# Token sums behind the attention output, both memory reciprocals in PSUM, K's last cast in halves

## The chip, the cores and the metric

The kernel runs on one core of one Trainium2 chip. The metric is the device time of one execution in microseconds. Before the change three runs took 749.27, 747.28 and 747.86 us, a median of 747.86.

## The reference

Two parts read the same x, 2048 tokens of 512 features, and a gate per token mixes them.

```python
def _A_ref(x, mem0, Wq, Wk, Wv, Wo, seg_len):      # 32 heads of 128, memory of 8 rows, segments of 32 tokens
    mem = mem0
    for s in range(n_seg):                          # 64 segments, one after the other
        h = jnp.concatenate([mem, xs], axis=1)      # 8 memory rows + 32 tokens
        q, k, v = ...                               # h times Wq, Wk, Wv
        scores = jnp.einsum('bhqe,bhke->bhqk', q, k) * scale
        scores = jnp.where(mask[None, None], scores, -1000000000.0)
        p = _softmax(scores, axis=-1)
        o = jnp.einsum('bhqk,bhke->bhqe', p, v)
        o = jnp.einsum('bhte,hed->btd', o, Wo)
        mem = o[:, :M, :].copy()                    # the next segment's memory
        outs.append(o[:, M:, :])
def _B_ref(x, w1, b1, w2, b2):
    y = _layernorm(x, axis=-1)
    h = _gelu(jnp.einsum('bsd,df->bsf', y, w1) + b1)
    return jnp.einsum('bsf,fd->bsd', h, w2) + b2
g = _sigmoid((x * gate_w).sum(-1, keepdims=True))
return g * a + (1 - g) * b
```

All weights and activations are bf16. The segments form a chain: segment s+1 needs the eight memory rows that segment s produced.

## The kernel before

The kernel has three stages. The first, to about 76 us, computes part B: layer norm, first matmul and gelu for all tokens, and the second matmul for seven of the sixteen blocks of 128 tokens. The hidden activations of the nine others are stored in DRAM (`h_dr`). The second stage is a loop over the 64 segments, here called steps 0 to 63; the last one leaves the loop half way. The third is the clean end: the last segment's output, sums that guard against overflow, and the last block of the result.

**One step.** The stationary operand `hT` has 32 columns: 24 tokens of the segment and 8 memory rows. The other 8 tokens of each segment ("left" tokens) depend on no memory, so for a whole block of four segments they are projected one block ahead, as side work. A matmul loads 32 columns of weights and uses one of four column groups of the array; four of them side by side are called a set here. A step on the matrix engine (PE) is:

1. Q and K in halves of 16 heads, order Q0, K0, Q1, K1 (`qk_unit`, L129), into the PSUM banks `U[0], U[2], U[1], U[3]`. ScalarE (ACT) casts each half to bf16 (`qk_cast`, L134), VectorE (DVE) transposes it into `QT` or `KT` (`qk_tr`, L138).
2. `scores(s, 0)` (L267, L271) of heads 0 to 15 into the bank `SbF`; ACT makes the exponentials `E` of them (L828).
3. V's first half into `X1` and one set of V's second half into `X2` (`v_unit`, L148); ACT casts V (`v_cast`, L834).
4. `xsums(E, 0)` (L715) sums the exponentials of the token queries over the keys; `msum(0)` (L816) does so for the memory queries of heads 0 to 15.
5. `scores(s, 1)` of heads 16 to 31 into `U[0]`, which need K1; the rest of V; `msum(1)` (L278, L281).
6. The attention output `av` (L291, L296): E times V, into all four `U` banks, first heads 0 to 15, then 16 to 31.
7. The memory rows' projection `wo_pass` (L160) into `X2`, cast to `w` (L752), and `new_mem` (L761), whose three results DVE casts into the next `hT` (L763).

Only the memory queries are normalised before `av`. `mnorm` on DVE reduces the sums (first half only, L823), takes the reciprocal (L824) and multiplies it into E's last 16 columns (L825). `RP` is the list of the two places where these reciprocals are kept: the first in the PSUM bank `SbF`, the second in the SBUF tile `RS`. The token queries are normalised behind `av`: `recip_x` takes the reciprocal of their sums (L726, L727), stores it to DRAM (`r_dr`, L730), reads it back broadcast to all partitions (`Rb`, L733), and in the next step GpSimd (POOL) multiplies it with the raw output (`x_norm`, L745) into `UT` and `UL`. `wo_pass` of that step needs this `UT`. Behind the reciprocal DVE also copies both `RP` into `R` (L735) and puts the mask back into `SbF` (L260).

**Side work.** PE is filled with work that is on no chain: the next block's left tokens or the last block's left projection (the generator `fill`, taken in units by `run(n)`: `W1` = 2 units before `av`, `W2` behind it, `W3` behind the projection, then one each between the parts of `new_mem`), and halves of the deferred second MLP matmul (`mlp_halves`, L689: 4 matmuls of 256 columns into the bank `W`), taken by `next(mlp)`. Each `hm` tile serves two halves. `hm_load` orders as many new tiles as have been used since the last call; it stands in `recip_x` between the store and the broadcast, on the same queue (SP). In step 2 the fill is MLP work alone, `mlp_units`, two halves to a unit.

**What sets the order.** The program is written out by hand (`manual_schedule`): each engine runs its instructions in the order of the source, and semaphores that the framework derives from overlapping tiles hold an instruction until what it needs is done. The SP queue takes DMAs in order too, and one that waits holds those behind it.

Of the kernel before, what the change touches and what calls it, by code (L numbers as in the profile page):

```python
# [9 lines left out]
FP32 = mybir.dt.float32  # L10
BF16 = mybir.dt.bfloat16
# [17 lines left out]
def kernel(ctx, tc, A_x, A_mem0, A_Wq, A_Wk, A_Wv, A_Wo, A_seg_len, B_x, B_w1, B_b1, B_w2, B_b2, gate_w, out):  # L29
    nc = tc.nc  # L30
    P = 128
# [100 lines left out]
    def qk_cast(bk):  # L132
        Tb = ew.tile([P, 8, 32, 2], BF16, tag="Tb", bufs=3, name="Tb")
        nc.scalar.copy(out=Tb[:], in_=bk.rearrange("p (a b e) -> p a e b", a=8, b=2))  # L134
        return Tb

    def qk_tr(Tb, dst, hf, c0=0):
        nc.vector.transpose(out=dst[:, 8 * hf:8 * hf + 8, c0:c0 + 32, :].rearrange("p a r b -> p a (r b)").bitcast(FP32),  # L138
                            in_=Tb[:].rearrange("p a e b -> p (a e b)").bitcast(FP32))
# [6 lines left out]
    def v_unit(bk, G, vb, kc):  # L146
        for j in range(4):
            nc.tensor.matmul(bk[32 * j:32 * j + 32, :], lhsT=G[:, kc, :], rhs=Wv5[:, kc, 4 * vb:4 * vb + 4, j, :],  # L148
                             start=(kc == 0), stop=(kc == KC - 1), tile_position=(0, 32 * j))
# [65 lines left out]
    def wo_left(T, bk):  # L215
        for n in range(NW):
            wo_group(bk, UL[T % 2], n)
            if n < NW - 1:
                yield

        def ca():
            wl = cw.tile([P, Dm], BF16, tag="wl", name="wl")
            nc.scalar.copy(out=wl[:], in_=bk[:])
            wls[T] = wl
        act_q.append(ca)
        yield
# [24 lines left out]
                              in_=QL[T % 2][:].bitcast(FP32).rearrange("p a (l s) b -> p a l s b", s=SPT)[:, :, :, si])  # L251


    RS = ep.tile([P, 32], FP32)
    RP = [SbF[:, 336:368], RS[:]]


    def mask_put(i2):
# [25 lines left out]
    def av(s, V, E):  # L284
        T, si = divmod(s, SPT)
        Uv = [U[j][:, 0:NG * 40].rearrange("p (i q) -> p i q", q=40) for j in range(4)]
        for i2 in range(2):
            for i in range(4 * i2, 4 * i2 + 4):
                for j in range(4):
                    q = slice(32 * j, 32 * j + 32)  # L290
                    nc.tensor.matmul(Uv[j][:, i, :], lhsT=V[q, i, :], rhs=E[q, i, 8:48],  # L291
                                     start=(i == 0), stop=False, skip_group_check=True, tile_position=(32 * j, 0))
            for j in range(4):
                q = slice(32 * j, 32 * j + 32)
                lo = slice(4 * i2, 4 * i2 + 4)
                nc.tensor.matmul(Uv[j][:, lo, :].rearrange("p i (a b) -> p i a b", b=8)[:, :, 0:5:4, :], lhsT=VP[T % 2][q, si, i2, :],  # L296
                                 rhs=E[q, lo, :].rearrange("p i (a b) -> p i a b", b=8)[:, :, 0:7:6, :],
                                 start=False, stop=True, skip_group_check=True, tile_position=(32 * j, 0))
# [329 lines left out]
    def run(n):  # L628
        for _ in range(n):
            next(fill, None)  # L630
# [5 lines left out]
    def side(T, si):  # L636
        gens = []
        if si == 2:
            gens = [wo_left(T - 1, X1) if T >= 1 else mlp_units(8)]
        elif T + 1 == NT:  # L640
            gens = [mlp_units(4)] if si < 2 else []
        else:
            gens = [[left_qk(T + 1, 0, 0, X1), left_qk(T + 1, 1, 0, U[3])], [left_qk(T + 1, 0, 1, X1), left_qk(T + 1, 1, 1, U[3])], [],
                    [left_v(T + 1, 0, X1), left_v(T + 1, 1, U[3])]][si]
        return chain(*gens)
# [32 lines left out]
    def mlp_outs():  # L678
        while outs:
            mlp_out(outs.pop())  # L680
# [16 lines left out]
    def mlp_units(n):  # L697
        for _ in range(n):
            next(mlp, None)
            next(mlp, None)  # L700
            yield
# [10 lines left out]
    def xsums(E, h):  # L712

        for c in range(4):
            nc.tensor.matmul(xs[32 * c:32 * c + 32, h, 0:40], lhsT=BO[:, 0:P:4], rhs=E[:, 4 * h + c, 0:40],  # L715
                             start=False, stop=True, skip_group_check=True, tile_position=(0, 32 * c))
# [51 lines left out]
    for s in range(nseg):  # L768
# [20 lines left out]
        for n, (t, hf) in enumerate(QK4):  # L789
            bk = U[(0, 2, 1, 3)[n]]  # L790
            for kc in range(n == 1, KC):
                qk_unit(bk, hc, t, hf, kc)
                if n == kc == 0:
                    qk_unit(U[2], hc, *QK4[1], 0)
            if n == 0:
                flush(act_q, 9)
                flush(dve_q, 9)
            qk_tr(qk_cast(bk[:]), (QT, KT)[t], hf, LEFT * (1 - t))
            if n == 0:
                mask_put(1)  # L800
        V = cx.tile([P, NG, Dh], BF16, tag="V", name="V")
# [9 lines left out]
        def msum(i2):  # L811
            if i2:
                sums(U[3][:, 320:352].rearrange("p (i q) -> p i q", q=8), E[:, 4:8, :], 40, 48, 8, True)
                return
            for j in range(4):
                nc.tensor.matmul(U[1][32 * j:32 * j + 32, 320:384], lhsT=BO[:, 32 * j:32 * j + 32], rhs=E[:, 0:4, 40:56],  # L816
                                 start=True, stop=True, skip_group_check=True, tile_position=(0, 32 * j))

        def mnorm(i2):
            r, e = RP[i2], E[:, 4 * i2:4 * i2 + 4, 40:56].rearrange("p i (a q) -> p i a q", q=8)  # L820
            if i2 == 0:
                m = U[1][:, 320:384].rearrange("p (i a q) -> p i q a", i=4, a=2)
                nc.vector.tensor_reduce(out=r.rearrange("p (i q) -> p i q", q=8), in_=m, axis=AX.X, op=ALU.add)  # L823
            nc.vector.reciprocal(out=r, in_=U[3][:, 320:352] if i2 else r)  # L824
            nc.vector.tensor_tensor(out=e, in0=e, in1=r.rearrange("p (i q) -> p i q", q=8).unsqueeze(2).to_broadcast([P, 4, 2, 8]), op=ALU.mult)  # L825
# [10 lines left out]
        v_cast(0, 0)  # L836
        v_unit(X2, hc, 1, 0)
        if not last:
            xsums(E, 0)
            msum(0)  # L840
            mnorm(0)
        scores(s, 1)
        exps(1, 0)
        v_cast(0, 1)
        exps(1, 1)
        for kc in range(1, KC - 1):
            v_unit(X2, hc, 1, kc)
        if not last:
            if s:
                next(mlp, None)  # L850
            msum(1)
            mnorm(1)
        v_unit(X2, hc, 1, KC - 1)
        for h in range(2):
            v_cast(1, h)
        if last:
# [1 line left out]
        run(W1)  # L858
        if s:
            next(mlp, None)  # L860
        xsums(E, 1)
        recip_x(s)
        av(s, V, E)
        for j in (0, 2, 1, 3):
            nc.scalar.copy(out=UT[s % 2][:, j, :, 0:M], in_=U[j][:, 0:NG * 40].rearrange("p (i q) -> p i q", q=40)[:, :, 32:40])  # L865
        x_raw(s)
# [15 lines left out]
        mlp_outs()  # L882
        for _ in fill:
            pass
        if si == 3 and T + 2 < NT:
            left_x(T + 2)
        flush(dve_q, 9)
# [9 lines left out]
    for _ in out_sel(T - 1, X1):  # L897
        pass
    fill = wo_left(T, X2)
    run(3)  # L900
    nc.vector.reciprocal(out=R[:, nx], in_=SbF[:, 0:32 * NG])
    nc.scalar.activation(out=rmin[:, nx], in_=R[:, nx], func=ACTF.Copy, accum_out=tot[:, 3:4])
    ws[s - 1] = wo_pass(UT[s % 2])
    Rr = R[:, nx].rearrange("p (i q) -> p i q", q=32)
    nc.vector.tensor_tensor(out=E[:, :, 8:40], in0=E[:, :, 8:40], in1=Rr, op=ALU.mult)
    nc.vector.tensor_tensor(out=E[:, :, 0:8], in0=E[:, :, 0:8], in1=Rr[:, :, 0:8], op=ALU.mult)
# [176 lines left out]
```

## Time and profile before

| | us |
|---|---|
| median of three runs | 747.86 |
| the profiled execution | 750.09 |
| its span, first to last instruction | 748.2 |
| PE busy | 732.8 |
| ACT busy | 536.7 |
| DVE busy | 448.9 |
| POOL busy | 246.6 |

One execution was profiled. Rows of the timeline give start, duration, engine, line, operation, output and inputs, shape and count of merged instructions, and in brackets how long the engine had stood idle and what released it. `DVE KT L138 <- ACT Tb L134` in the waits means that DVE's instruction of line 138 waited for ACT's of line 134. Matmul rows overlap: a row's duration is how long one matmul takes from end to end, and the pace is read from the distance of starts. PEld is the weight load that goes ahead of a matmul. Rows of `windows` give busy times per engine and, behind them, the share of full speed at which the matrix engine's clock was granted. A step lasts about 10.2 us.

### The profile page before, as it was taken

Reading aid. Unit: us, or ns where it says so; the run is one execution under the profiler, and the core shown is the slowest. Engines: PE = TensorE matmul, PEld = TensorE weight load, DVE = VectorE, ACT = ScalarE, POOL = GpSimd, SP = SyncE. Lnnn points to the kernel's source line nnn. Section 1 sums busy time; section 2 is a strip of 40 time slices with the busy share of each in tenths; the row PEclk is TensorE's granted clock in tenths of the full one; section 3 lists DMA queues with packets and bytes.
Section 4 is the critical chain, followed back from the end, with each engine's and each line's share of the span. In section 5 each row is a group of like instructions: output and inputs, shape, how many; then the busy total and the mean of one; then the engine's idle time right before and its main releaser. Section 6 shows DMA issues by size and latency. Waiting matters only on the chain. (4 is left out here: it accounts for less than half of the span.)

```text
span 748.2 us, 44010 instructions
## 1 busy us (share of the span) xinstructions
PE 732.8 (98%) x19147; PEld 428.8 (57%) x19147; DVE 448.9 (60%) x1541; ACT 536.7 (72%) x1629; POOL 246.6 (33%) x515
## 2 busy tenths in 40 slices
PE   8999998999999999999999999999999999999997
PEld 5776554556565555555555555555555555555553
DVE  6877554656565555656565665556665656555554
ACT  6777765777777777777777777777777777777664
POOL 4001332332334333343234334243333343333331
PEclk9999999999999999999999999999999999999999
DMA  8999222222222323122321323231322313222221
GB/s 308 343 360 360 84 83 55 69 87 80 78 68 62 97 74 93 47 83 80 93 79 38 96 75 97 69 81 57 92 78 82 85 44 94 69 90 70 85 63 61
DMA packets 61944, 76.82 MB, mean 103 GB/s; under 512 B 26729, under 2 KB 51922, under 8 KB 60210
## 3 DMA queue, kind: packets, MB, share of 16 engines
q1 hardware_dynamic: 60802, 72.51, 31.1%
q8 instruction: 151, 2.47, 1.3%
q0 software_dynamic: 400, 0.92, 0.3%
q10 hardware_dynamic: 544, 0.52, 0.2%
q14 instruction: 47, 0.39, 0.2%
HBM read 60.21 MB, written 7.70 MB: 91 GB/s over the span
## 5 line engine op out<-in xcount | busy, mean ns | idle before, releaser
L134 ACT CAST Tb<-U 128x512 bf16<-128x512 f32 x288 | 168.8, 586 | 82.5 <-PE U L129 76.8
L745 POOL TENSOR_TENSOR UT<-XR,Rb 128x384 bf16<-128x384 bf16 x126 | 114.1, 927 | 324.6 <-DMA Rb<-r_dr 228.0
L129 PEld LDWEIGHTS <-hT 128*32 128x32 bf16 x4096 | 108.8, 97 | 97.8 <-issue 2.0
L129 PE MATMUL U<-Wq_sb,hT 128*32 128x512 bf16 x2048 | 145.9, 382 | 0.4 <-DVE hT L763 0.4
L129 PE MATMUL U<-Wk_sb,hT 128*32 128x512 bf16 x2048 | 145.2, 381 | 0.0
L148 PE MATMUL X<-Wv_sb,hT 128*32 128x512 bf16 x2048 | 142.9, 378 | 0.0
L160 PE MATMUL X<-Wo_sb,UT 128*32 128x512 bf16 x2016 | 120.8, 380 | 0.0
L834 ACT CAST V<-X 128x256 bf16<-128x256 f32 x256 | 88.7, 372 | 16.0 <-PE X L148 1.1
L138 DVE STREAM_TRANSPOSE QT<-Tb 128x256 f32<-128x256 f32 x128 | 57.0, 445 | 71.1 <-ACT Tb L134 70.9
L763 DVE CAST hT<-U 128x8 bf16<-128x8 f32 x126 | 20.8, 167 | 130.9 <-PE U L761 96.6
L160 PEld LDWEIGHTS <-UT 128*32 128x32 bf16 x2048 | 56.4, 96 | 55.7 <-issue 16.6
L721 ACT CAST XR<-U 128x256 bf16<-128x256 f32 x252 | 78.6, 438 | 0.0
L752 ACT CAST w<-X 128x128 bf16<-128x128 f32 x189 | 44.8, 310 | 41.7 <-PE X L160 41.0
L138 DVE STREAM_TRANSPOSE KT<-Tb 128x256 f32<-128x256 f32 x128 | 57.0, 445 | 25.9 <-ACT Tb L134 25.9
L737 POOL TENSOR_TENSOR racc<-racc,R 128x128 f32<-128x128 f32 x63 | 28.8, 457 | 105.7 <-DVE R L735 101.1
L148 PEld LDWEIGHTS <-hT 128*32 128x32 bf16 x2048 | 45.2, 95 | 20.6
L689 PE MATMUL W<-w_sb,hm 128*32 128x256 bf16 x728 | 50.5, 273 | 3.6 <-DMA hm<-h_dr 3.6
L865 ACT CAST UT<-U 128x64 bf16<-128x64 f32 x252 | 35.4, 227 | 25.9 <-PE U L296 25.9
L745 POOL TENSOR_TENSOR UL<-XR,Rb 128x128 bf16<-128x128 bf16 x126 | 51.5, 430 | 0.0
L809 ACT ACTIVATE E<-U 128x64 bf16<-128x64 f32 (+1 forms) x128 | 35.0, 273 | 9.3 <-PE U L271 0.4
L484 PEld LDWEIGHTS <-w_sb 128*128 128x128 bf16 (+1 forms) x352 | 34.1, 100 | 10.4
L160 PE MATMUL X<-Wo_sb,UL 128*32 128x512 bf16 x512 | 38.7, 379 | 1.0 <-POOL UL L896 1.0
(184 smaller groups left out, 1250.5 us busy)
## 6 DMA issues: line engine op xcount, KB each, us to landing
Rb<-r_dr SPq DMA_DIRECT2D x63, 512.0 KB, 3.9
Wv_sb<-in_A_Wv_dram SPq DMA_DIRECT2D x4, 1024.0 KB, 7.5
Wq_sb<-in_A_Wq_dram SPq DMA_DIRECT2D x4, 1024.0 KB, 8.5
Wk_sb<-in_A_Wk_dram SPq DMA_DIRECT2D x4, 1024.0 KB, 8.4
Wo_sb<-in_A_Wo_dram SPq DMA_DIRECT2D x4, 1024.0 KB, 12.6
VP<-VL SPq DMA_DIRECT2D x64, 64.0 KB, 3.7
hm<-h_dr SPq DMA_DIRECT2D x91, 32.0 KB, 2.6
c<-c_dr SPq DMA_DIRECT2D x16, 128.0 KB, 4.6
```

The source lines that it names most:

```text
L129: nc.tensor.matmul(bk[32 * j:32 * j + 32, :], lhsT=G[:, kc, :], rhs=W5[t][:, kc, h0:h1, j, :], start=(kc == 0), stop=(kc == KC - 1), tile_ ...
L134: nc.scalar.copy(out=Tb[:], in_=bk.rearrange("p (a b e) -> p a e b", a=8, b=2))
L138: nc.vector.transpose(out=dst[:, 8 * hf:8 * hf + 8, c0:c0 + 32, :].rearrange("p a r b -> p a (r b)").bitcast(FP32), in_=Tb[:].rearrange("p ...
L148: nc.tensor.matmul(bk[32 * j:32 * j + 32, :], lhsT=G[:, kc, :], rhs=Wv5[:, kc, 4 * vb:4 * vb + 4, j, :], start=(kc == 0), stop=(kc == KC - ...
L160: nc.tensor.matmul(bk[32 * c:32 * c + 32, :], lhsT=U_[:, j, i, :], rhs=Wo_sb[:, 4 * i + j, :], start=(n == 0), stop=(n == NW - 1), tile_po ...
L689: nc.tensor.matmul(W[32 * c:32 * c + 32, cc], lhsT=hm[:, 32 * c:32 * c + 32], rhs=w2_sb[:, fc, cc], start=(fc == 0 and h == 0), stop=(fc = ...
L721: nc.scalar.copy(out=XR[:, j], in_=U[j][:, 0:NG * 40].rearrange("p (i q) -> p i q", q=40)[:, :, 0:32])
L745: nc.gpsimd.tensor_tensor(out=out[:, :, 4 * h:4 * h + 4, o:o + b - a], in0=XR[:, :, 4 * h:4 * h + 4, a:b], in1=Rb[:, h, :, :, r:r + b - a] ...
L752: nc.scalar.copy(out=w[:, a:b], in_=bk[:, a:b])
L809: nc.scalar.activation(out=E[:, 4 * i2:4 * i2 + 4, c], in_=Sb[i2][:, :, c], func=ACTF.Exp, scale=scale)
L834: nc.scalar.copy(out=V[:, i0:i0 + 2, :].rearrange("p i e -> p (i e)"), in_=(X1, X2)[vb][:, 256 * h:256 * h + 256])
L865: nc.scalar.copy(out=UT[s % 2][:, j, :, 0:M], in_=U[j][:, 0:NG * 40].rearrange("p (i q) -> p i q", q=40)[:, :, 32:40])
```

## The change

- The second memory reciprocal is kept in `SbF` next to the first; the tile `RS` is gone.
- K1 is cast and transposed in two halves of eight heads each, both casts first, then both transposes.
- `xsums(E, 0)` moves from before `msum(0)`, and `xsums(E, 1)` from before `av`, to behind `av`; `recip_x` follows them there.
- The last set of V's second half moves ahead of `msum(1)`; the MLP half that stood before `msum(1)` moves behind it.
- The fill of step 2 has six units, not eight; one MLP half is added at the end of step 3 and three at the end of step 4.
- In the clean end three sets of the leftover projection move from before the last `wo_pass` to behind it.

```diff
-    RS = ep.tile([P, 32], FP32)
-    RP = [SbF[:, 336:368], RS[:]]
+    RP = [SbF[:, 336 + 32 * i:368 + 32 * i] for i in range(2)]
...
-            gens = [wo_left(T - 1, X1) if T >= 1 else mlp_units(8)]
+            gens = [wo_left(T - 1, X1) if T >= 1 else mlp_units(6)]
...
-            qk_tr(qk_cast(bk[:]), (QT, KT)[t], hf, LEFT * (1 - t))
+            if n < 3:
+                qk_tr(qk_cast(bk[:]), (QT, KT)[t], hf, LEFT * (1 - t))
+            else:
+                Tb = ew.tile([P, 8, 32, 2], BF16, tag="Tb", bufs=3, name="Tb")
+                for a in (0, 4):
+                    nc.scalar.copy(out=Tb[:, a:a + 4], in_=bk[:, 64 * a:64 * a + 256].rearrange("p (a b e) -> p a e b", a=4, b=2))
+                for a in (0, 4):
+                    nc.vector.transpose(out=KT[:, 8 + a:12 + a].rearrange("p a r b -> p a (r b)").bitcast(FP32),
+                                        in_=Tb[:, a:a + 4].rearrange("p a e b -> p (a e b)").bitcast(FP32))
...
         if not last:
-            xsums(E, 0)
             msum(0)
             mnorm(0)
         scores(s, 1)
         exps(1, 0)
         v_cast(0, 1)
         exps(1, 1)
-        for kc in range(1, KC - 1):
+        for kc in range(1, KC):
             v_unit(X2, hc, 1, kc)
         if not last:
+            msum(1)
+            mnorm(1)
             if s:
                 next(mlp, None)
-            msum(1)
-            mnorm(1)
-        v_unit(X2, hc, 1, KC - 1)
...
-        xsums(E, 1)
+        av(s, V, E)
+        for h in range(2):
+            xsums(E, h)
         recip_x(s)
-        av(s, V, E)
...
+        for _ in range({SPT - 1: 1, SPT: 3}.get(s, 0)):
+            next(mlp, None)
+            mlp_outs()
...
-    run(3)
     nc.vector.reciprocal(out=R[:, nx], in_=SbF[:, 0:32 * NG])
     nc.scalar.activation(out=rmin[:, nx], in_=R[:, nx], func=ACTF.Copy, accum_out=tot[:, 3:4])
     ws[s - 1] = wo_pass(UT[s % 2])
+    run(3)
```

The order on DVE in an ordinary step, from Q1's transpose to the mask, before. Names are outputs and inputs, then the shape; `DVE_49` and the like are the semaphores of the engines, `DMAHW0_49` one of the DMAs.

```order
L138 STREAM_TRANSPOSE QT<-Tb 128x8x32 [waits Activation_49]
L138 STREAM_TRANSPOSE KT<-Tb 128x256 [waits Activation_49]
L823 TENSOR_REDUCE SbF<-U_119 128x32 [waits DVE_49,PE_49,Activation_49]
L824 RECIPROCAL SbF<-SbF 128x32 [waits DVE_49]
L825 TENSOR_TENSOR E<-E,SbF 128x4x16 [waits DVE_49]
L824 RECIPROCAL RS<-U_121 128x32 [waits PE_49]
L825 TENSOR_TENSOR E<-E,RS 128x4x16 [waits DVE_49,Activation_49]
L726 TENSOR_REDUCE SbF<-SbF 128x2x8 [waits PE_49]
L727 RECIPROCAL R<-SbF 128x64 [waits DMAHW0_49,DVE_49,Pool_49]
L735 COPY R<-RS 128x32
L735 COPY R<-SbF 128x32
L260 CAST SbF<-MkF 128x336 [waits DVE_49]
```

The same place after.

```order
L138 STREAM_TRANSPOSE QT<-Tb 128x8x32 [waits Activation_49]
L804 STREAM_TRANSPOSE KT<-Tb 128x128 [waits Activation_49] x2
L830 TENSOR_REDUCE SbF<-U_119 128x32 [waits DVE_49,PE_49,Activation_49]
L831 RECIPROCAL SbF<-SbF 128x32 [waits DVE_49]
L832 TENSOR_TENSOR E<-E,SbF 128x4x16 [waits DVE_49]
L831 RECIPROCAL SbF<-U_121 128x32 [waits DVE_49,PE_49]
L832 TENSOR_TENSOR E<-E,SbF 128x4x16 [waits DVE_49,Activation_49]
L725 TENSOR_REDUCE SbF<-SbF 128x2x8 [waits DVE_49,PE_49]
L726 RECIPROCAL R<-SbF 128x64 [waits DMAHW0_49,DVE_49,Pool_49]
L734 COPY R<-SbF 128x32 x2
L259 CAST SbF<-MkF 128x336 [waits DVE_49]
```

The second memory reciprocal (`SbF<-U_121`) now also waits on DVE's own semaphore: the DVE instruction it names is the product in front of it, which reads the same PSUM bank.

On PE the sequence from V's second half to the attention output, before; weight loads and repeats are left out.

```order
L148 MATMUL X_123<-Wv_sb,hT_86 32x512
...
L715 MATMUL SbF<-E,BO 32x40
...
L816 MATMUL U_119<-E,BO 32x64
...
L267 MATMUL U_118<-QT,KT 32x40
...
L278 MATMUL U_121<-E,BO 32x32
...
L160 MATMUL X_122<-Wo_sb,UL_1373 32x512
...
L291 MATMUL U_118<-E,V 128x40
...
L296 MATMUL U_118<-E,VP_94 128x4x2x8
```

And after.

```order
L148 MATMUL X_123<-Wv_sb,hT_86 32x512
...
L823 MATMUL U_119<-E,BO 32x64
...
L266 MATMUL U_118<-QT,KT 32x40
...
L277 MATMUL U_121<-E,BO 32x32
...
L160 MATMUL X_122<-Wo_sb,UL_1372 32x512
...
L290 MATMUL U_118<-E,V 128x40
...
L295 MATMUL U_118<-E,VP_94 128x4x2x8
...
L714 MATMUL SbF<-E,BO 32x40
```

The token sums (`SbF<-E,BO 32x40`, half of them before `msum` and half before `av`) all stand behind the attention output now.

## The prediction

> **What bounds the kernel now.** I read the page's engine table first, then the waits, then the timeline of one ordinary step engine by engine, and last the two places where the waits view shows the matrix engine standing still.
>
> ```profile
> PE 732.8 (98%) x19147; PEld 428.8 (57%) x19147; DVE 448.9 (60%) x1541; ACT 536.7 (72%) x1629; POOL 246.6 (33%) x515
> PE W L689 <- DMA hm<-h_dr: 3.6, 3, 2.4
> ```
>
> PE looks full, and its largest wait is 3.6 us for the MLP's `hm` tiles. But matmul rows overlap, so short stops hide inside that 98%. They appear when the starts of PE rows are compared with what those rows should need. This is the step that begins near 424 us:
>
> ```profile
> 425.96 0.21 PE L816 MATMUL U<-E,BO 128*32 128x64 bf16 x4
> 426.07 0.28 PE L267 MATMUL U<-QT,KT 128*32 128x40 bf16 x16
> 426.22 0.60 PE L148 MATMUL X<-Wv_sb,hT 128*32 128x512 bf16 x8
> 426.81 0.38 PE L148 MATMUL X<-Wv_sb,hT 128*32 128x512 bf16 x4
> 427.83 0.35 PE L291 MATMUL U<-E,V 32*128 32x40 bf16 x16
> 428.02 0.19 PE L296 MATMUL U<-E,VP 32*128 32x64 bf16 x4
> 428.14 0.61 PE L129 MATMUL X<-Wq_sb,GL 128*32 128x512 bf16 x8
> 428.60 0.40 PE L160 MATMUL X<-Wo_sb,UT 128*32 128x512 bf16 x4
> ...
> 426.28 0.23 DVE L823 TENSOR_REDUCE SbF<-U 128x32 f32<-128x64 f32 x1 [0.27 <-PE U L816]
> 426.55 0.37 DVE L824 RECIPROCAL SbF<-SbF 128x32 f32<-128x32 f32 x1
> 426.95 0.22 DVE L825 TENSOR_TENSOR E<-E,SbF 128x64 bf16<-128x64 bf16 x1
> 427.09 0.35 DVE L824 RECIPROCAL RS<-U 128x32 f32<-128x32 f32 x1
> 427.54 0.23 DVE L825 TENSOR_TENSOR E<-E,RS 128x64 bf16<-128x64 bf16 x1
> 427.85 0.20 DVE L726 TENSOR_REDUCE SbF<-SbF 128x16 f32<-128x32 f32 x1
> ...
> 424.95 0.59 ACT L134 CAST Tb<-U 128x512 bf16<-128x512 f32 x1 [0.23 <-PE U L129]
> 425.43 0.36 ACT L828 ACTIVATE E<-SbF 128x224 bf16<-128x224 f32 x1
> 427.25 0.65 ACT L834 CAST V<-X 128x256 bf16<-128x256 f32 x2
> ```
>
> A set of four 512-column matmuls takes 0.22 us (two sets in 0.60, less the 0.38 of one). Two stops follow. The scores of L267 start 0.11 us after msum (L816), which needs about 0.03: about 0.08 is the wait for K's transpose. The attention output's second half (L291 at 427.83, ending in L296 at 428.02) takes 0.19 where its sixteen small matmuls need about 0.10. In this step V's last casts end that wait, at 427.25 + 0.65 = 427.90; the second memory product ended at 427.54 + 0.23 = 427.77. In other steps the vector engine ends it:
>
> ```profile
> 406.63 0.44 DVE L825 TENSOR_TENSOR E<-E,RS 128x64 bf16<-128x64 bf16 x1
> 406.18 0.81 POOL L745 TENSOR_TENSOR UL<-XR,Rb 128x128 bf16<-128x128 bf16 x2
> 407.12 0.28 PE L291 MATMUL U<-E,V 32*128 32x40 bf16 x16
> 407.36 0.40 PE L148 MATMUL X<-Wv_sb,GL 128*32 128x512 bf16 x4
> ...
> L825 DVE TENSOR_TENSOR E<-E,RS 128x64 bf16<-128x64 bf16 x63 | 17.8, 283 | 6.6
> L825 DVE TENSOR_TENSOR E<-E,SbF 128x64 bf16<-128x64 bf16 x63 | 13.9, 221 | 2.1
> ```
>
> The same product costs 221 ns with its reciprocal in PSUM and 283 ns on average with it in SBUF. The one at 406.63 took 0.44 while POOL worked, and ended at 407.07; PE went on 0.05 later, and 0.29 after that end came the first matmul behind the attention output.
>
> **The change, part by part.** *Memory reciprocals.* With `RS` gone, the second product should cost 0.22 always: 63 x (283 - 226) ns = 3.6 us of excess go away, 226 being what an undisturbed one takes (0.23 above). The lead of V's casts, 427.90 against 427.77, already hid part, so between nothing (excess spread evenly) and 3.6 reaches PE; the excess sits in few long rows like 406.63, so I take 3.1.
>
> But the second reciprocal now writes the PSUM tile that the first product reads, and the new order makes it wait for that product. Today it starts at 427.09, 0.14 after the product's start and 0.08 before its end. What such a wait costs is seen one row on: 427.09 + 0.35 = 427.44, and the product that waits for it starts at 427.54, so 0.10. The walk through this step after the change:
>
> - msum starts 0.03 earlier, at 425.93, since one set of token sums no longer stands ahead of it. E must be ready. K's last cast becomes two: the two V casts take 0.65, so the second starts 0.28 after the first. Then E starts at 424.95 + 0.28 + 0.28 = 425.51 and ends at 425.87, plus 0.05 to PE: just in time.
> - Reduce, reciprocal and first product keep their distances: product from 426.92 to 427.14.
> - Wait 0.10, second reciprocal 427.24 to 427.61 (0.37, as the PSUM-to-PSUM row), wait 0.10, second product 427.71 to 427.93.
> - First matmul behind the attention output at 427.93 + 0.29 = 428.22. Here the two sets of token sums now stand, 0.05; the two fill sets follow at 428.27, 0.43 long, and the memory projection (L160) starts at about 428.71-428.72 instead of 428.60.
>
> So an ordinary step becomes 0.12 longer: 63 x 0.12 = +7.6. If the wait costs 0.03, as between the reduce and the reciprocal (426.51 to 426.55), it is 63 x 0.05 = +3.2; if E comes 0.03 late, 63 x 0.15 = +9.5. I take 0.12, since the row it comes from has the same kind of wait. Less the 3.1: **+4.5**.
>
> A rule of the Trainium skill speaks against this price: "VectorE: DVE Perf Modes", section "The DRAIN you can't avoid", says the next operation does not start until the pipe is empty and that semaphores between operations cost nothing extra. Here a reciprocal starts 0.08 before the product's end, so the trace does not agree for this pair; by the rule the term would be -4.4, as rival A works out, instead of +7.6.
>
> *K in halves, V's last set earlier.* K's transpose in halves ends the 0.08 wait at L267, and V's casts end about 0.25 earlier because X2 is complete earlier. Both only bring PE sooner to the attention output, where it now waits for the second product until 427.98: price 0, cover about 0.3 us of that wait. Were the cover gone, both would show as gain: 63 x 0.08 = 5 us at most. ACT pays 0.08 a step, inside its idle time.
>
> *Token sums and their reciprocal later.* The reduce of L726 moves from 427.85 to about 428.55, so the r_dr store, the hm loads queued behind it on SP, the Rb broadcast and POOL's products of the next step all move by 0.7, or about 0.6 against PE. What waits last is the memory projection:
>
> ```profile
> 693.23 1.81 POOL L745 TENSOR_TENSOR UT<-XR,Rb 128x384 bf16<-128x384 bf16 x2 [6.14 <-ACT E L828]
> 695.88 0.37 PEld L160 LDWEIGHTS <-UT 128*32 128x32 bf16 x12 [0.31 <-POOL UL L745]
> ```
>
> 693.23 + 1.81 = 695.04 leaves 0.84, the shortest lead of an ordinary step. It shrinks to about 0.25. Two early, disturbed steps could run short: +0.3; bounds 0 and 2.
>
> *Side units.* Two units fewer in step 2, one half more after step 3, three after step 4:
>
> ```profile
> 103.81 0.19 PE L761 MATMUL U<-SelM,w 128*32 128x8 bf16 x4
> 104.89 0.40 PE L689 MATMUL W<-w_sb,hm 128*32 128x256 bf16 x8 [0.89 <-DMA hm<-h_dr]
> 105.90 0.39 PE L129 MATMUL U<-Wq_sb,hT 128*32 128x512 bf16 x4
> ...
> 114.94 0.62 PE L148 MATMUL U<-Wv_sb,GL 128*32 128x512 bf16 x8
> 117.96 0.29 PE L689 MATMUL W<-w_sb,hm 128*32 128x256 bf16 x4 [2.41 <-DMA hm<-h_dr]
> core 0: us, PE busy (x) PEld busy (x) DVE busy (x) ACT busy (x) POOL busy (x), PEclk, DMA share, GB/s
> 119.01:122.43 3.42, 3.42 (x40) 1.37 (x32) 0.98 (x4) 1.37 (x3) 1.21 (x2) 0.50 0.48 148
> ...
> 410.11 0.19 PE L761 MATMUL U<-SelM,w 128*32 128x8 bf16 x4
> 410.68 0.40 PE L129 MATMUL U<-Wq_sb,hT 128*32 128x512 bf16 x4
> ```
>
> In the new order each `hm` used was loaded in an earlier step; before, step 2 and step 3 each used one whose load was issued in the same step. From the new memory's first matmul to the next Q is 105.90 - 103.81 = 2.09 in step 2 and 0.57 in an ordinary one, and without the last two units it is still about 0.57: -1.5. The four halves return later, four times 0.11: +0.4. In step 3 PE should go on at 114.94 + 0.43 = 115.37 instead of 117.96: -2.6. After that stop the granted clock was 0.50 for 3.42 us: -1.7. Sum **-5.4**; bounds -3.7 (no half clock to save) and -5.8.
>
> On this half clock, "TensorE: Matmul & The Clock Gate", section "What's actually happening", says the clock falls after an idle window of about 3.4 us, and that the window runs free of the kernel. The trace shows a stop of 2.6 us sufficing. By the rule as stated the 1.7 would not be this wait's, and the sum would be 1.7 higher.
>
> *Clean end.* The last step's projection now stands ahead of the leftover one:
>
> ```profile
> 736.38 0.40 PE L234 MATMUL X<-wl,SelL 128*32 128x512 bf16 x4
> 737.74 0.83 PE L160 MATMUL X<-Wo_sb,UL 128*32 128x512 bf16 x12 [0.96 <-POOL UL L896]
> 734.87 1.80 POOL L745 TENSOR_TENSOR UT<-XR,Rb 128x384 bf16<-128x384 bf16 x2 [6.66 <-DMA Rb<-r_dr]
> ```
>
> PE idles from 736.60 to 737.74 for POOL's memset. Afterwards it waits only for UT, 736.67 plus the 0.7 of delay, about 737.4. One of the projection's eight sets runs before: **-0.5**, bounds 0 and -1.1.
>
> Sum: +4.5 - 5.4 - 0.5 + 0.3 = -1.1 us.
>
> **The rivals.** *A, the wait between product and reciprocal is free* (this is the rule cited above). The second product ends at 427.74, 0.19 sooner than in my walk; an ordinary step is 63 x 0.07 = 4.4 shorter than before, the 3.1 is kept, and -5.4 - 0.5 + 0.3 come on top: 13 us less, 734.8. For it: nothing is computed from the product. Against it: the 0.10 row.
> *B, it costs 0.03, or the step has slack I don't see.* +3.2 - 3.1 - 5.6 = -5.5: 742.4. For it: 426.51 to 426.55. Against it: there only one thing is waited for; the new reciprocal waits for PE and for its own engine.
> *C, slower: the `hm` waits only move.* At the start of the MLP's deferred part the loads now leave SP 0.7 later, and a half that waits in step 4 or 5 costs what 117.96 cost. If the loads miss by the same 2.6, -5.4 becomes about 0 and the sum is +4.3: 752.2. It decides when a load lands more than one step (10 us) after its issue; the load waited for at 117.96 was issued within the same step, whose span is 14.5 us, and landed well inside it, which speaks against it.
> *D, slower: POOL's products come late.* It decides once Rb comes 0.85 later against PE rather than 0.6; at 1.6 a third of the steps wait and it costs some 7 us: 753.8.
>
> **How the numbers follow.** The profiled execution took 750.09 us, 748.2 of it span and 1.9 around it; the median of the runs shown is 747.86, 2.2 lower. Whether the timed runs all fell to half clock is not shown, so I count 1.3 of its 1.7: -0.7 in all, **747.2 us**. A difference of 0.3%, 2.2 us, is about what measuring this kernel can tell from none.
> Chances: my case 0.57, with its own range from 744.8 to 750.6 out of the bounds above; A 0.05, B 0.23, C 0.09, D 0.06. Of my case 0.06 lies below 745.6 and 0.05 above 750.1. So faster is 0.05 + 0.23 + 0.06 = 0.34, slower 0.09 + 0.06 + 0.05 = 0.20, same 0.46. The range is stretched from my case to B's 742.4 and a little past it, **742.0 to 750.6**, and leaves out A, C and D, 0.20.
>
> **What the profile after would show.** Right, if the second reciprocal starts about 0.32 after the first product's start; if E,SbF products are all near 221 ns; if ordinary steps are 0.1 longer and PE's second half of the attention output starts 0.05 after the second product; if L688 waits for no `hm` and no half clock stands near 119 us. Wrong, if V's casts still end the wait, if POOL's UT products end behind the fill, or if E comes late to msum.

## The result, and the profile after

The changed kernel took 751.47 us, the median of five runs (751.28 to 752.83), against 748.15 us before, also of five (747.28 to 750.04). The ratio is 1.0055, with a 95% interval from 1.0034 to 1.0076: slower, and above the range of the forecast. A second set of runs gave 1.0058 (1.0036 to 1.0081). The execution that was profiled took 752.83 us, 751.1 of it span; the one before had 750.09 and 748.2.

The engine table, and the group of the memory products, of the changed kernel:

```profile
PE 737.0 (98%) x19147; PEld 420.9 (56%) x19147; DVE 462.8 (62%) x1605; ACT 534.6 (71%) x1693; POOL 247.6 (33%) x515
L832 DVE TENSOR_TENSOR E<-E,SbF 128x64 bf16<-128x64 bf16 x126 | 27.9, 221 | 9.0 <-ACT V L841 0.5
```

All 126 products now take about 221 ns: the long ones are gone, 31.7 us before and 27.9 now. PE is 4.2 us busier all the same. The timeline of one ordinary step after the change (the one whose memory sums start at 434.47):

```profile
434.47 0.20 PE L823 MATMUL U<-E,BO 128*32 128x64 bf16 x4
434.50 0.26 PE L266 MATMUL U<-QT,KT 128*32 128x40 bf16 x16
...
435.05 0.37 DVE L831 RECIPROCAL SbF<-SbF 128x32 f32<-128x32 f32 x1
435.27 0.18 PE L277 MATMUL U<-E,BO 128*32 128x32 bf16 x4
...
435.45 0.22 DVE L832 TENSOR_TENSOR E<-E,SbF 128x64 bf16<-128x64 bf16 x1
...
435.50 0.66 ACT L841 CAST V<-X 128x256 bf16<-128x256 f32 x2
...
435.77 0.37 DVE L831 RECIPROCAL SbF<-U 128x32 f32<-128x32 f32 x1
...
436.25 0.22 DVE L832 TENSOR_TENSOR E<-E,SbF 128x64 bf16<-128x64 bf16 x1
...
436.52 0.28 PE L290 MATMUL U<-E,V 32*128 32x40 bf16 x16
...
436.76 0.25 PE L714 MATMUL SbF<-E,BO 128*32 128x40 bf16 x8
...
437.27 0.60 PE L160 MATMUL X<-Wo_sb,UT 128*32 128x512 bf16 x8
```

The first product ends at 435.67 and the second reciprocal starts 0.10 later, though its sums (L277) were issued at 435.27; it ends at 436.14, and 0.11 later the second product starts. PE's second half of the attention output starts at 436.52, 0.05 behind that product. V's casts have been over since 436.16. The scores (L266) start 0.03 behind the memory sums: K's transpose is no longer waited for.

To compare kernels, each step was given a mark, the start of V's first set of the second half (into `X2`), and the distances were read from the traces. Medians over the 63 steps, in ns behind the mark (the first row: behind the first product's end; the last row: over the steps from 4 on):

| | before | after |
|---|---|---|
| second reciprocal starts | -82 | +103 |
| second product ends | 2054 | 2214 |
| V's last cast ends | 2170 | 1904 |
| last matmul of the attention output starts | 2303 | 2393 |
| memory projection starts | 2877 | 3024 |
| step, mark to mark | 10189 | 10323 |

And the span, cut at the marks (us):

| | to the mark of step 0 | step 0 to 4 | step 4 to 62 | behind it |
|---|---|---|---|---|
| before | 77.4 | 47.4 | 599.4 | 24.1 |
| after | 77.4 | 42.1 | 607.3 | 24.3 |

So 5.3 us went where the side units were moved, 7.9 came in over the ordinary steps, and the end stood still, but for 0.2.

### The profile page after: what moved, and what is told of

It is laid out like the page before. It is cut to its first block, busy times and chain, and to the rows that moved or that the text cites. A ratio compares the mean times of both kernels' runs of the same rounds, so it can differ in the third digit from the quotient of the medians.

```text
span 751.1 us, 44264 instructions
## 1 busy us (share of the span) xinstructions
PE 737.0 (98%) x19147; PEld 420.9 (56%) x19147; DVE 462.8 (62%) x1605; ACT 534.6 (71%) x1693; POOL 247.6 (33%) x515
## 5 line engine op out<-in xcount | busy, mean ns | idle before, releaser
L134 ACT CAST Tb<-U 128x512 bf16<-128x512 f32 x224 | 131.5, 587 | 62.5 <-PE U L129 56.8
L129 PEld LDWEIGHTS <-hT 128*32 128x32 bf16 x4096 | 108.5, 96 | 96.2 <-DVE hT L762 0.7
L148 PE MATMUL X<-Wv_sb,hT 128*32 128x512 bf16 x2048 | 132.2, 378 | 0.0
L160 PEld LDWEIGHTS <-UT 128*32 128x32 bf16 x2048 | 54.1, 96 | 56.3 <-issue 11.9
L148 PEld LDWEIGHTS <-hT 128*32 128x32 bf16 x2048 | 47.3, 95 | 25.6
L802 ACT CAST Tb<-U 128x256 bf16<-128x256 f32 x128 | 41.4, 375 | 16.3 <-PE U L129 16.3
L804 DVE STREAM_TRANSPOSE KT<-Tb 128x128 f32<-128x128 f32 x128 | 37.6, 312 | 11.7 <-ACT Tb L802 11.7
L290 PEld LDWEIGHTS <-V 32*128 32x128 bf16 x2048 | 27.4, 91 | 29.4 <-issue 17.1
L290 PE MATMUL U<-E,V 32*128 32x40 bf16 x2048 | 38.6, 178 | 2.6 <-DVE SbF L831 0.2
```

Of the source, the lines that this page charges most:

```text
L160: nc.tensor.matmul(bk[32 * c:32 * c + 32, :], lhsT=U_[:, j, i, :], rhs=Wo_sb[:, 4 * i + j, :], start=(n == 0), stop=(n == NW - 1), tile_po ...
L802: nc.scalar.copy(out=Tb[:, a:a + 4], in_=bk[:, 64 * a:64 * a + 256].rearrange("p (a b e) -> p a e b", a=4, b=2))
```

## The experiments

All ratios are to the kernel before, run on the same chip; the changed kernel has 1.0055 and 1.0058.

| run | median, us | ratio, 95% interval |
|---|---|---|
| psum_only | 770.62 | 1.0307 (1.0284 to 1.0330) |
| u3 | 766.64 | 1.0251 (1.0228 to 1.0275) |
| rs_back | 749.05 | 1.0005 (0.9989 to 1.0022) |
| side_only | 744.72 | 0.9962 (0.9944 to 0.9981) |
| swap | 752.57 | 1.0057 (1.0036 to 1.0078) |
| recips_first | 746.61 | 0.9973 (0.9956 to 0.9989) |
| sums_first | 743.19 | 0.9922 (0.9902 to 0.9941) |
| sums_first_whole_k | 746.23 | 0.9962 (0.9949 to 0.9976) |
| after_again | 751.69 | 1.0058 (1.0036 to 1.0081) |
| no_side | 755.55 | 1.0111 (1.0088 to 1.0134) |
| after_whole_k | 749.47 | 1.0027 (1.0010 to 1.0044) |
| after_old_end | 752.29 | 1.0075 (1.0052 to 1.0098) |
| sums_first_old_v | 742.82 | 0.9933 (0.9910 to 0.9957) |
| pad16, pad32, pad48 | 752.80, 753.44, 759.76 | one execution each |

### Where the second reciprocal is kept

Four runs move it. Three of them, against the changed kernel, in which they all replace the same line:

```diff
 rs_back
-    RP = [SbF[:, 336 + 32 * i:368 + 32 * i] for i in range(2)]
+    RS = ep.tile([P, 32], FP32)
+    RP = [SbF[:, 336:368], RS[:]]
 u3
-    RP = [SbF[:, 336 + 32 * i:368 + 32 * i] for i in range(2)]
+    RP = [SbF[:, 336:368], U[3][:, 352:384]]
 swap
-    RP = [SbF[:, 336 + 32 * i:368 + 32 * i] for i in range(2)]
+    RS = ep.tile([P, 32], FP32)
+    RP = [RS[:], SbF[:, 368:400]]
```

> The changed kernel with the second memory reciprocal back in the SBUF tile RS; all other parts stay. Theory 1: the wait is gone as in the run u3, but the second product meets POOL again, its mean rises from 222 to about 283 ns, and 63 x 0.06 = 3.6 us or a little less come back: about 743, range 740 to 746. Theory 2: the products' long rows come on top of what the change costs otherwise: 753 to 755.

> The changed kernel, with the second memory reciprocal kept in the free columns 352 to 383 of the PSUM bank U[3] (where its sums stand) instead of SbF. It stays in PSUM, but no longer waits for the first product. Theory 1 (the added wait on DVE is what made the change slower): the second reciprocal starts about 0.08 us before the first product's end again instead of 0.10 behind it, the second product ends some 0.19 earlier in each step, and no product rises above 0.23 us; 63 x 0.19 = 12 less than the changed kernel's 751.5, so about 740, range 737 to 743. Theory 2 (the wait is hidden, and the lost time lies in later POOL products or in single stalls of PE that the new order brings): 750 to 752, no change.

> The changed kernel with the two places exchanged: the first memory reciprocal in the SBUF tile RS, the second in SbF. The second reciprocal then writes a bank that the first product does not read, and nothing else is queued behind either. Theory 1 (the wait of the second reciprocal for the first product costs 0.19 us a step): it starts 0.08 before the first product's end again; the first product now meets POOL and costs 0.06 to 0.13 more on average, as the second one did with RS; so steps are 0.06 to 0.13 shorter, 743.5 to 747.5 us. Theory 2 (the reciprocal's wait is free): no shorter than the changed kernel, 751 to 755.

The long second products came back in `rs_back`, longer than in the kernel before; in `swap` the first product took its place. The groups of the products in `rs_back`, then in `swap`:

```profile
L833 DVE TENSOR_TENSOR E<-E,RS 128x64 bf16<-128x64 bf16 x63 | 24.1, 382 | 6.6
```

```profile
L833 DVE TENSOR_TENSOR E<-E,RS 128x64 bf16<-128x64 bf16 x63 | 28.3, 449 | 6.6
```

The mean was 283 ns in the kernel before. The reason is that the token sums, and with them POOL's products of the next step, stand later in the new order, so that POOL works just when the product with the SBUF reciprocal runs. One such pair in `rs_back`:

```profile
444.89 1.80 POOL L745 TENSOR_TENSOR UT<-XR,Rb 128x384 bf16<-128x384 bf16 x2 [6.59 <-ACT V L842]
...
445.48 0.42 DVE L833 TENSOR_TENSOR E<-E,RS 128x64 bf16<-128x64 bf16 x1
```

The two POOL products take 0.9 each; the first ended near 445.79, and DVE's product 0.11 behind it. In `rs_back` 39 second products take over 232 ns and in `swap` 48 first ones, and every one of them overlaps a POOL product. The Trainium skill, "SBUF — State Buffer", section "SBUF: two separate sides", calls the port pair that VectorE and GpSimd share an exclusive lock, held for a whole instruction, taken by a VectorE operation with two SBUF inputs when GpSimd's operation reads SBUF. The traces agree: up to 906 ns in `rs_back` and 996 in `swap` with both inputs in SBUF, at most 224 with one in PSUM, in every run.

So both theories were off by the size of that contention, and the two runs' times do not tell them apart: in `swap` the second reciprocal starts 76 ns before the first product's end, as Theory 1 said, and the 180 ns won go to the first product, whose median is 401. The price of the wait can be read in the single steps of `rs_back` in which POOL does not stretch the product. In the steps 33 and 36 the second product takes 226 and 225 ns, ends at 2030 and 2032, and the memory projection starts at 2838 and 2841, 0.18 us before the changed kernel's 3024.

`u3` gives the same on DVE (second reciprocal 78 ns before the first product's end, no product above 223 ns, second product's end 2034), but loses it all: its step takes 10.69 us. The attention output's first half writes all four `U` banks, and its fourth matmul, the first into `U[3]`, now starts 0.05 behind the second product's end, at 2088 ns instead of 1941. ACT and PE stand behind DVE's copy of the reciprocals, which reads `U[3]` too:

```profile
424.91 0.21 ACT L871 CAST UT<-U 128x64 bf16<-128x64 f32 x1 [0.72 <-DVE R L734]
```

```profile
PE U L129 <- ACT XR L720: 6.5, 28, 0.2
```

This was a poor experiment for its question: the wait that it took away came back on another bank.

### Only the reciprocals, and only the order of DVE

`psum_only` is the kernel before with the two lines of `RP` from the change.

> The kernel before with this one part of the change: both memory reciprocals in SbF. Theory 1: the second product ends 0.18 to 0.19 later in an ordinary step, 63 x 0.18 = +11, less the 3.3 of long products: about 756, range 753 to 758. Theory 2 (the wait costs nothing, PSUM only removes long products): 745.

It cost almost three times what the walk said, for a reason that neither theory had. The chain of waits of PE:

```profile
PE SbF L714 <- DVE E L824: 17.2, 60, 0.4
```

In the old order the second set of token sums stands ahead of the attention output and writes `SbF`; with the second reciprocal there it must wait for the second product. PE starts the attention output at 2452 instead of 1968. So the PSUM place and the moved token sums are one edit: the first is only bearable with the second. The steps of this run are also the most even: from step 8 to 62 they take only 0.5 us more than their medians add up to, each of the four kinds of step with its own, against 3.3 in the kernel before.

`recips_first` keeps both reciprocals in `SbF` and only changes the order on DVE:

```diff
             nc.vector.reciprocal(out=r, in_=U[3][:, 320:352] if i2 else r)
-            nc.vector.tensor_tensor(out=e, in0=e, in1=r...)
+            for k in range(2 * i2):
+                r, e = RP[k], ...
+                nc.vector.tensor_tensor(out=e, in0=e, in1=r...)
```

> The changed kernel, both reciprocals in SbF, but on DVE the second reciprocal stands ahead of the first product, so that the two reciprocals and then the two products follow each other and nothing waits for a product. If msum(1) is there when the first reciprocal ends, and the second product starts 0.08 before the first one's end: second product's end 0.18 earlier, 63 x 0.18 = 11.6: 740. If the second reciprocal has to wait for PE, or the product does not overlap: 0.08 a step, 746. If the wait never cost anything: 751.

```profile
433.38 0.18 PE L277 MATMUL U<-E,BO 128*32 128x32 bf16 x4
...
433.69 0.37 DVE L831 RECIPROCAL SbF<-U 128x32 f32<-128x32 f32 x1 [0.18 <-PE W L688]
433.99 0.29 PE L688 MATMUL W<-w_sb,hm 128*32 128x256 bf16 x4
434.10 0.35 DVE L834 TENSOR_TENSOR E<-E,SbF 128x64 bf16<-128x64 bf16 x2
```

The two products overlap: 0.35 together, where one takes 0.22. The second reciprocal is held by PE now, 0.18 behind the first, and starts 1.13 us behind the memory sums instead of 1.31. The second product ends at 2094 instead of 2214, the memory projection starts at 2939 instead of 3024, and the kernel is 0.8% faster than the changed one with the same instructions on every engine. Not all of that is the wait: of the 6.0 us between the two profiled spans 3.7 lie between the marks of step 4 and step 62, and 1.3 behind the latter, where DVE goes on sooner at the very end (see the idle instructions below). What the ordinary steps gain is the wait of the reciprocal for the product. This is the middle case of the expectation, 746.

### Token sums ahead again, K whole again, V's set back

`sums_first` is `rs_back` with `xsums` and `recip_x` ahead of `av` again. `sums_first_whole_k` has K's last cast in one piece as well, `sums_first_old_v` has V's last set and the MLP half in their old places instead.

```diff
 sums_first, beside the lines of rs_back
-        av(s, V, E)
         for h in range(2):
             xsums(E, h)
         recip_x(s)
+        av(s, V, E)
```

> The changed kernel with RS back and the token sums, their reciprocal and the r_dr store ahead of the attention output again; K's halves, V's set, the side units and the clean end stay. Theory: the second product no longer waits and POOL's products come as early as before, so its mean falls back from 382 to about 283 ns; V's casts, which ended the attention output's wait in the kernel before (last matmul 2303 ns after the step's mark, second product's end 2054), end earlier, so PE leaves the attention output about 0.1 us earlier: 63 x 0.1 = 6 below the run side_only: 739, range 737 to 742. Rival (the long second products end the wait anyway): 743 to 745, as side_only.

> As sums_first, with K's last cast and transpose in one piece again. Theory (the 0.08 us that PE waits for K's transpose is covered by its later wait for the second product): within 1.5 us of sums_first. Rival (the cover is gone in this order): 63 x 0.08 = 5 us slower than sums_first.

> The run sums_first with V's last set (and the MLP half ahead of msum(1)) in the old places. Theory: V's casts end 0.22 later, 2.12 us after the step's mark, and end the attention output's wait again, its last matmul 0.04 to 0.06 later: 63 x 0.05 = 3 us slower than sums_first, ratio to the kernel before 0.996. Rival (the second product ends the wait in most steps anyway, as the prediction had it: price 0): as sums_first, 0.992.

| ns behind the mark, medians | side_only | sums_first | sums_first_whole_k | sums_first_old_v |
|---|---|---|---|---|
| second reciprocal, behind the first product's end | -82 | -76 | +39 | -82 |
| second product ends | 2053 | 2037 | 2146 | 2019 |
| V's last cast ends | 2170 | 1903 | 2011 | 2085 |
| last matmul of the attention output | 2303 | 2216 | 2326 | 2220 |
| memory projection | 2879 | 2811 | 2912 | 2801 |

`sums_first` is the best of all, together with `sums_first_old_v`: 5.8 us below the kernel before (0.9922), and faster than both kernels. Its second products are back at 297 ns:

```profile
L833 DVE TENSOR_TENSOR E<-E,RS 128x64 bf16<-128x64 bf16 x63 | 18.7, 297 | 6.6
```

Against `rs_back` it shows what the late token sums cost when the reciprocal is in SBUF: 0.8%, 6 us.

K's halves are worth 0.4%, 3.0 us, in this order; between the marks of step 4 and step 62 it is 4.5 us, and 1.2 go back behind them, where `sums_first` has the later end that is told below. With K whole the scores of heads 16 to 31 start at 350 instead of 244, `msum(1)` is late, and the second reciprocal waits for PE. V's set in the old place changes nothing that can be measured (0.9933 against 0.9922, the intervals overlap): its casts end at 2085, and the attention output leaves at the same time.

### The side units

`side_only` is the kernel before with the side units of the change; `no_side` is the changed kernel without them.

> The kernel before with the side units alone (six units in step 2, one more MLP half after step 3, three after step 4). Theory 1: the two waits for hm go and the half clock behind them, -3.7 to -5.8, so about 742.7, range 742 to 744.5. Rival (the waits only move to steps 4 and 5): 748, no change.

> The changed kernel without the side units (eight units in step 2, no added MLP halves). The prediction's term: the two waits for hm come back in steps 2 and 3, +3.7, and the half clock behind them in some executions, +1.7: 755 to 757. By the run side_only, which gained 2.8: 754.3.

They are worth 0.38% one way and 0.53% the other: 2.8 and 4.0 us. In the trace of `no_side` PE waits again:

```profile
PE W L688 <- DMA hm<-h_dr: 2.9, 2, 2.1
```

Its steps 0 to 4 take 46.6 us instead of 42.1, and its granted clock falls to half at 117.4. In `psum_only`, whose side work is the old one, PE waits 2.3 us for `hm` as well, but no half clock follows and the four steps take 45.6, its own longer steps included. So two waits are there in all three traces of the old order, the half clock in two of them.

### K whole and the old end in the changed kernel

> The changed kernel with K's last cast and transpose in one piece. The prediction's term (price 0): the second reciprocal starts 1305 ns after the step's memory sums in the changed kernel, behind the first product; msum(1), 0.1 later with K in one piece, would be done by 1240: still covered, so 751 to 753, no change. Rival, by the runs sums_first and sums_first_whole_k (3.0 us apart): 754 to 755.

> The changed kernel with the clean end in its old order. The prediction's term: +0.5. By the traces: from the memory projection of step 62 to the last matmul 16.0 us in the new order, 16.2 to 17.3 in the old: +0.2 to +1.3, 751.7 to 753.5. If the move brings nothing: 751.5, and 16.0 in the trace.

With K whole the changed kernel's ordinary step stays as it is: second product's end 2214, memory projection 3025. The price 0 was right in this order. The kernel even became 0.3% faster, which neither theory had; what differs is told below.

The old end costs 0.17%, 1.3 us. From the memory projection of step 62 to the last matmul it takes 17.48 us, against 16.01 in the changed kernel and 17.30 in the kernel before.

### A second trace, and idle instructions

> The changed kernel again, for a second trace of it. In the first one, single steps (2, 10, 12, 16, 20, 24, 49, 53, 56, 60) reach the memory projection 0.1 to 0.7 us late, 4.6 us in all, in stops of PE that wait for nothing the profile shows, and the last write took 5.3 us from PE's last matmul to the end of the span. Theory X (these come by chance in each execution): other steps, another sum, 1 to 5 us, and an end of 3.7 or 5.3. Theory Y (the new order causes them): the same steps with the same sizes within 0.1. The median time stays at 751 to 753.

> The changed kernel with 16 idle DVE instructions (a memset of one unused column) ahead of the loop; nothing else differs. Theory P (the place of DVE's code decides): the end from the last matmul to the end of the span is 3.7 us in at least one of pad16, pad32 and pad48, and the DVE stops of steps 52, 56 and 60 move to other steps. Theory Q (the new order decides): 5.3 us in all three, and the stops stay at 52, 56 and 60.

> As pad16 with 32 idle instructions, and the same two theories.

> As pad16 with 48 idle instructions, and the same two theories.

```diff
 pad16 (pad32 and pad48 likewise)
+    pad = lp.tile([P, 1], FP32)
+    for _ in range(16):
+        nc.vector.memset(pad[:], 0.0)
     mask_put(0)
```

`after_again` showed some of both. Five late steps were new (7, 26, 35, 41, 48), seven came back (9, 10, 16, 24, 52, 56, 60), and the sum of the late steps was 3.4 us instead of 4.6. Of those that came back, 52, 56 and 60 had the same 0.14, 0.35 and 0.35, and the end again took 5.3 us. In the new trace as in the first, DVE pauses there for about 0.35 us (0.14 in step 52) beyond what it waits for. With 16 idle DVE instructions ahead of the loop such pauses stand in the steps 27 and 60, with 32 in 10, 14 and 59, with 48 in 30 and 45. The pauses hang on where DVE's code lies.

The other late steps come in the main from stops of PE, and these do not wander as freely as their sizes suggest. One of them, in step 10 of the changed kernel:

```profile
184.28 0.61 PE L160 MATMUL X<-Wo_sb,UL 128*32 128x512 bf16 x6 [0.31 <-issue]
```

When the starts of matmuls are compared with those of other steps of the same kind, the steps 7, 10, 14, 16, 24 and 33 have a stop ahead of the same matmul in both traces, of other sizes: 0.69 and 0.42 us in step 10, 0.55 and 0.22 in step 16, 0.07 and 0.67 in step 7. The stop of step 10 is there in all eight traces that have this order on PE in the step, at 0.33 to 0.69, and idle DVE instructions do not move it. Counted along PE's program these six matmuls are 894, 1150, 639, 2300 and 2556 apart, which are all multiples of about 127.8. The kernel before stops ahead of the same matmuls by number in steps 7, 14 and 16, by 0.26, 0.21 and 1.09. So the places belong to the program; why a stop is long in one execution and short in the next is not shown.

So does the end. The timeline's last matmul in the changed kernel, and then, by the view of the last branch's line (L975), what DVE's own sequencer did there (count, durations in ns, first and last start in us):

```profile
745.77 0.24 PE L949 MATMUL U<-w,SelI 128*32 128x192 bf16 x1 [0.41 <-ACT w L945]
```

```profile
core 0 of [0], span 751.1 us
...
L975 DVEq COMPARE_BRANCH  x1: 76/76/76, 746.9 to 746.9; - x1
...
L975 DVEq EVENT_SEMAPHORE  x1: 21/21/21, 750.0 to 750.0; - x1
```

The same two views of `pad32`, where the branch is in line 978:

```profile
747.76 0.24 PE L952 MATMUL U<-w,SelI 128*32 128x192 bf16 x1 [0.41 <-ACT w L948]
```

```profile
core 0 of [0], span 751.6 us
...
L978 DVEq COMPARE_BRANCH  x1: 76/76/76, 748.9 to 748.9; - x1
...
L978 DVEq EVENT_SEMAPHORE  x1: 21/21/21, 749.5 to 749.5; - x1
```

From the last matmul to the end of the span it is 5.3 us in the one and 3.8 in the other. DVE's first instruction behind the branch comes 3.0 us after it, or 0.6. It came 2.9 to 3.1 us after it in the changed kernel, `pad16`, `rs_back` and `sums_first`, and 0.6 in the kernel before, `swap`, `recips_first`, `after_whole_k`, `pad32` and `pad48`. Theory P held: the place of DVE's code decides. Why a place is a slow one is not shown.

`pad48` reached the mark of step 0 5.9 us later than the changed kernel, with the clock at half from 80.1, so that its total says nothing about the change.

## Why the prediction was wrong

The forecast was 747.2 us and no measurable difference; it is 751.5 and slower. Every sign that I had named for being right came true in the profile; they tested the walk through a step, and not what the steps add up to. On the profiled pair my terms gave -1.1 us and 2.8 came, and 3.5 of these 3.9 lie in the ordinary steps. Term by term:

**The step that failed: "Less the 3.1".** The walk through the ordinary step was right: the second reciprocal starts 0.32 behind the first product's start, the second product ends 2214 - 2054 = 0.16 later, the memory projection starts 0.15 later where I had 0.12, and the step is 0.134 longer, 58 x 0.134 = 7.8 us between the marks of step 4 and step 62. From this I took off 3.1 us for the long products. They did disappear, 3.8 us of them on DVE. But between those marks the time rose by 7.9 us, as much as the longer step gives alone, where my terms gave (7.6 - 3.1 + 0.3) x 58 / 63 = 4.4.

Two things took the place of the 3.1. First, not all of it was on the path. In the kernel before, the 17 products above 240 ns between those marks exceed 226 ns by 3.0 us in all, but in their steps the attention output's last matmul comes only 2.0 us late, each step counted with no more than its product's excess. V's casts, which end 0.12 behind an ordinary second product, hide the start of every excess. I had named that cover and then took almost the whole sum. Second, the changed kernel has other single stops. Against the median of each of the four kinds of step, the late steps from 8 to 62 hold 3.3 us in the kernel before, long products included, and 2.4 and 3.3 in the two traces of the changed one: of the 3.1, between nothing and 1.0 is found. Part of these stops is identified: the DVE pauses that hang on the place of the code, which are 0.8 us of steps 52, 56 and 60, and are missing in `after_whole_k`, whose 58 steps take 605.7 instead of 607.3 us. With other numbers of idle instructions the 58 steps took 605.6 to 608.5. The rest are stops of PE that wait for nothing the profile shows, most of them at fixed matmuls of the program; what sets their size stays open.

**The price of the wait, 0.10 with both ends: right.** It measured 0.103 behind the product's end, against 0.082 ahead of it. The undisturbed steps of `rs_back` show that the whole 0.18 is the wait; `recips_first` got 0.12 of it back, since there PE holds the second reciprocal. Rival A fell; rival B's 0.03 fell too, and it held 0.23 of the chances. Of the section that I cited for rival A, the Trainium skill's "VectorE: DVE Perf Modes", "The DRAIN you can't avoid", one statement disagrees with these traces, that a semaphore costs nothing extra. The same paragraph goes on to say that a next operation that is not held starts earlier, which the overlap of 0.082 bears out and which I had left out.

**Side units, -5.4: right for the profiled pair, too much for the median.** Steps 0 to 4 took 5.3 us less, and no `hm` wait or half clock is left. By the medians the gain is 2.8 to 4.0, near the bound that I had without the half clock, 3.7; of that clock I had counted 1.3 of 1.7.

**Clean end, -0.5: the matmuls gained more, the program nothing.** They end 17.30 - 16.01 = 1.3 us sooner, beyond my bound of 1.1. DVE's code behind the last branch came 2.4 us later and gave back 1.6. I had no term for that, and no view of the kernel before could have shown it.

**K's halves and V's set, price 0: right here.** The cover, PE's wait for the second product, holds in the changed order; in `sums_first`, where the product comes earlier, it is gone, and K's halves are worth 4.5 us in the steps, of the 5 that I named.

**Token sums later, +0.3: right as far as the changed kernel goes, though blind to the tie.** POOL's products ended behind the projection's start in two steps of 63, by 0.3, and in the second trace in one, by 0.8. That the later products meet the second product, so that a reciprocal in SBUF would have cost 382 ns, I did not see; nor that PSUM in the old order would stop PE at the token sums. I priced the parts of the change as if each could stand alone.

The profiled pair adds up: -5.3 + 7.9 + 0.2 = 2.8 us, the difference of the two spans. The medians differ by 3.3, in part because the profiled execution before lies 1.9 above its median and the one after 1.4. Rivals C and D, with which I had filled the slower side, did not happen.

## What to carry to other kernels

A small tile that is kept in a bank with others takes on the waits of that bank: here the second reciprocal waited for a product that reads other columns of it, and in `psum_only` PE's token sums waited for the second product. So the place of a tile and the order around it are one decision and must be priced together. When a wait is unavoidable, put an instruction that depends on neither side between the two: here the same instructions in another order were worth 0.8%, about two thirds of it in the steps. A gain that consists of a few long rows should not be counted in full: some of it is covered by whatever else ends the same wait, and other single stops lie on the same path.

## What the runs showed of the hardware

- Two DVE instructions with no wait between them overlap by 0.08 us (reciprocal behind product, product behind product); with a wait on DVE's own semaphore the second starts 0.10 behind the first one's end. The difference, 0.18, is most of a 0.22 us product.
- The place of an instruction in the program can cost time: 3.0 instead of 0.6 us for DVE's first instruction behind the last branch, and pauses of about 0.35 us in the loop. Sixteen idle instructions left the end as it was, 32 and 48 shortened it by 1.5 and 1.2 us. In a kernel of 750 us that alone is 0.2%, as much as most of the parts of this change.
- PE has such places too: stops of 0.07 to 1.09 us ahead of the same matmuls in several traces, multiples of about 127.8 matmuls apart.
- The same half clock that followed a `hm` wait in two traces did not follow a wait of nearly the same length in a third (`psum_only`, longest 1.8 us, against 2.1 in `no_side` and 2.4 before).
